# Attention followed by a spectral mixing layer: one prefetched weight tile per stage, and the first output unit's last products whole

## The chip, the cores and the metric

The kernel runs on one core of a Trainium2 chip. The metric is the device time of one execution in microseconds (us), from the first to the last instruction and what the device adds around them. The kernel before takes 450.63 us, the median of three runs (450.61 to 451.6); the profiled execution spans 448.3 us.

## The reference, cut to what matters

Two layers run in one launch. The first is attention with a sliding window of 128 and a bias that falls off with distance, for 8 batches, 8 heads, 576 tokens and 64 channels per head. The second takes the result x (8 x 576 x 512), goes to the frequency domain along the tokens, multiplies each of the 64 lowest modes by its own complex 512 x 512 matrix, comes back, adds x, and puts a last 512 x 512 product through a ReLU.

```python
scores = scale * np.matmul(q, k.transpose(0, 1, 3, 2))
scores = np.where(mask, scores + bias[None], -1000000000.0)
...
x = attn_out.transpose(0, 2, 1, 3).reshape(B, S, H * D)
X = np.fft.rfft(x, axis=1)
Xr, Xi = np.real(X[:, :64]), np.imag(X[:, :64])
Yr = np.einsum('bmd,mde->bme', Xr, w_r) - np.einsum('bmd,mde->bme', Xi, w_i)
Yi = np.einsum('bmd,mde->bme', Xr, w_i) + np.einsum('bmd,mde->bme', Xi, w_r)
Y[:, :64] = Yr + 1j * Yi
y = np.fft.irfft(Y, n=S, axis=1)
u = x + y
out = u + np.maximum(u @ w_ch, 0.0)
```

The weights w_r and w_i are 2 x 64 matrices of 1.05 MB each in f32. One of them (the imaginary part of mode 0) has no effect and is not loaded, so 127 are read, and each is used once. The inputs q, k and v together are 28.3 MB.

## The kernel before

The attention is a software pipeline of 16 units (batch, half of the heads). In each stage, the parts of several units run side by side. Three loads per unit (q, k and v, f32) come on the queue of SP; each raw buffer has two places, and the load of unit u + 2 is ordered right after the cast of unit u:

```python
def cast(self, u, w):
    src = self.loaded.pop((w, u))
    if w == "v":
        ...
            nc.vector.tensor_copy(self.vb[u % 2][...], src[row, :2])
        nc.vector.tensor_copy(self.vt[u % 2][64:96, :, :, :D], src[64:96, 2])
    else:
        ...
        nc.vector.tensor_copy(dst.rearrange("p j e d -> p e j d"), src)
    self.load(w, u + 2)
```

While the attention runs, the first weights are already fetched. They come on the queue of GpSimd (POOL), which casts them to bf16 on the way. A gate keeps them from all coming at once: POOL copies one element of the attention's result of the stage before into a small tile, and so waits for it before it orders the next weights. `AHEAD` says how many tiles are ordered behind the gate of a stage. `LATER` adds tiles at the end, into the raw buffers that q, k and v no longer need.

```python
AHEAD = {1: 1, 2: 1, 4: 2, 5: 1, 7: 1, 8: 1, 10: 1, 11: 1, 12: 2, 13: 2}
LATER = {13: 2, 14: 2, 15: 3}
EARLY, NWA, NWB, AGAIN = 14, 6, 2, 8
...
    if stage in AHEAD:
        if stage:
            b, g = at.units[stage - 1]
            nc.gpsimd.tensor_copy(gate[:1, :1], x[:1, b, 0, 256 * g : 256 * g + 1])
        load_w(AHEAD[stage], early, True)
    if stage in LATER:
        load_w(LATER[stage], None, True)
```

One early tile is loaded before the stages, so with the 13 of `AHEAD` there are 14, one for each place of the pool `early`.

Then comes the stream: the remaining weights arrive on the queue of SP in f32 (eight of them once more through POOL in bf16), and TensorE multiplies each by the spectrum XC, four products of 512 columns per weight, into `acc`. SP can order the first of them when the attention's buffers, whose place they take, are free.

```python
for a in range(4):
    nc.tensor.matmul(into[...], lhsT=window[a], rhs=w[a], ...)
```

The end turns the last group of modes into rows `yq` (token side) and, through w_ch, `yw` (channel side), patches them with small DMAs into the spectra Z and ZW, and then makes 18 output units. Each unit j has a pair of PSUM tiles `mm` (channel side, goes through the ReLU on ACT into r) and `yy` (token side), and o = yy + r on DVE. For the first units the last rows are added by a product of their own, so that they need not wait for the patch:

```python
def last_rows(ps, j, rows, c=slice(0, DM)):
    st = units[j][1]
    for n in range(2):
        nc.tensor.matmul(ps[:, n, c], lhsT=FM[:, n, st * P : (st + 1) * P],
                         rhs=rows[:, c], start=False, stop=True, skip_group_check=True)

def activate(j):
    if j == 0:
        last_rows(yys[0][0], 0, heads["yq"])
        for c in sides:
            last_rows(mms[0][0], 0, heads["yw"], c)
    elif j in FIRST:
        last_rows(mms[j][0], j, heads["yw"])
    else:
        begin(j)
        channels(j)
    ...
        nc.scalar.activation(r[:, c], mm[:, c], AF.Relu)
```

`begin(j)` and `channels(j)` start the pair `mm` (4 products from XW, lines 717 of the profile, then 4 from ZW, line 638). `add_tokens` and `finish_tokens` do the same for `yy` (lines 766 and 775). The last rows and the order of the first units before:

```python
zls = [zps.tile([P, DM], FP32, tag=f"z{i}", name=f"zl{i}") for i in range(2)]
for ets in ((0, 1), (2, 3)):
    for zl, c in zip(zls, sides):
        for et in ets:
            nc.tensor.matmul(zl[:, c], lhsT=yT[:, et], rhs=wch[:, et, c],
                             start=(et == 0), stop=(et == 3))
for zl, c, copy in zip(zls, sides, (nc.scalar.copy, nc.vector.tensor_copy)):
    copy(yw[:, c], zl[:, c])
...
activate(0)
...
take(1)
begin(1)
channels(1)
channel_rows = partial(patch, rows=yw, g=LAST, dst=lambda b: ZW[:, b // 2, 1])
channel_rows([(nc.sync, 0), (nc.sync, 1)] + [(nc.gpsimd, b) for b in range(2, B)])
...
for step in ("f0 a1 f1 a2 a3 f2 a7 f7 a9 a5 ...").split():
    {"a": activate, "f": finish}[step[0]](int(step[1:]))
```

Of the kernel before, what the change touches and what calls it, by code (L numbers as in the profile page):

```python
# [10 lines left out]
FP32 = mybir.dt.float32  # L11
# [4 lines left out]
PSUM = bass.MemoryType.PSUM  # L16
# [4 lines left out]
P = 128  # L21
# [20 lines left out]
    ("mask", 1, 0), ("value", 1, 1), ("evacuate", "k", -1), ("mask", 0, 0), ("exp", 3, 0),  # L42
    ("transpose", "q", -2), ("evacuate", "q", -2), ("score", 1, -1), ("norm", 1, 1),
)


class _Halves:


    def __init__(self, tiles):  # L50
        self.tiles = tiles

    def __getitem__(self, key):
        return self.tiles[key[1]][(key[0], *key[2:])]


class _Scratch:
# [352 lines left out]
def kernel(  # L410
# [10 lines left out]
    nc = tc.nc  # L421
    ctx.enter_context(tc.manual_schedule(engines=ALL | {SP}))
    B, H, S, _ = q.shape
    NM, DM, _ = moe_w_r.shape
    AHEAD = {1: 1, 2: 1, 4: 2, 5: 1, 7: 1, 8: 1, 10: 1, 11: 1, 12: 2, 13: 2}
    LATER = {13: 2, 14: 2, 15: 3}
    EARLY, NWA, NWB, AGAIN = 14, 6, 2, 8
    HM = NM // 2
# [41 lines left out]
    with ExitStack() as actx:  # L470
        at = _Attention(tc, actx, q, k, v, (ident, F, FT), x, XC, raw)
        n = len(at.units)
# [50 lines left out]
        for stage in range(min(lags), n + max(lags)):  # L523
# [6 lines left out]
            if stage == 3:  # L530
                at.inverse_table()
# [8 lines that stand above are left out]
    with ExitStack() as mctx:  # L540
# [6 lines left out]
        first = todo_w[0]  # L547
# [4 lines left out]
        ps = pctx.enter_context(tc.tile_pool(name="fps", bufs=1, space=PSUM))  # L552
        heads, free, idle = {}, [], []
# [24 lines left out]
        def late_channels(zw, yT, yw, c):  # L578
            for et in range(4):
                nc.tensor.matmul(zw[:, c], lhsT=yT[:, et], rhs=wch[:, et, c],  # L580
                                 start=(et == 0), stop=(et == 3))
            nc.scalar.copy(yw[:, c], zw[:, c])
# [111 lines left out]
        POOLED, HALVES, FIRST = (3, 4, 9, 11, 13, 14, 15), (0, 1, 2, 3, 7, 12), (0, 1)  # L694
        mms, yys, rs = {}, {}, {}

        def pair(tag, slot=0):
            return heads[tag][slot].tile([P, 2, DM], FP32, tag=tag, name=tag)
# [5 lines left out]

        def begin(j):

            if j not in mms:
                slot = idle.pop(0)
                mms[j] = pair("mm", slot), slot
            mm = mms[j][0]  # L710
            for n in range(2):
                if units[j][1] == FULL:
                    nc.tensor.matmul(mm[:, n], lhsT=pairs, rhs=XW[:, j, n],
                                     start=True, stop=False, skip_group_check=True)
                    continue
                for row in range(2):
                    nc.tensor.matmul(  # L717
                        mm[ROWS[row], n], lhsT=ident[ROWS[n], ROWS[n]],
                        rhs=XW[ROWS[n], j, row], start=True, stop=False, skip_group_check=True,
                    )  # L720

        def channels(j):

            mm, b, st = mms[j][0], *units[j]
            for n in range(2):
                if st == FULL:
                    nc.tensor.matmul(mm[:, n], lhsT=FC, rhs=ZW[:, b // 2 + n, 1],
                                     start=False, stop=True, skip_group_check=True)
                    continue
                for row in range(2):  # L730
                    spread(mm[:, n], row, b + n, 1, st, row)

        def last_rows(ps, j, rows, c=slice(0, DM)):

            st = units[j][1]
            for n in range(2):
                nc.tensor.matmul(ps[:, n, c], lhsT=FM[:, n, st * P : (st + 1) * P],  # L737
                                 rhs=rows[:, c], start=False, stop=True, skip_group_check=True)

        def parts(j):  # L740
            return (slice(0, 1), slice(1, 2)) if j in HALVES else (slice(0, 2),)

        def activate(j):

            if j == 0:
                last_rows(yys[0][0], 0, heads["yq"])
                for c in sides:
                    last_rows(mms[0][0], 0, heads["yw"], c)
            elif j in FIRST:
                last_rows(mms[j][0], j, heads["yw"])  # L750
            else:
                begin(j)
                channels(j)
            mm, slot = mms.pop(j)
            r = rs[j] = heads["out"].tile([P, 2, DM], FP32, tag="r", name="r")
            for c in (0, 1) if j == 0 else parts(j):
                nc.scalar.activation(r[:, c], mm[:, c], AF.Relu)  # L757
            idle.append(slot)
            if j in POOLED:
                nc.gpsimd.tensor_tensor(out=r, in0=r, in1=token_tiles(j), op=ALU.add)  # L760
# [25 lines left out]
        def finish(j):  # L786

            b, st = units[j]
            if j > 0:
                if j not in yys:  # L790
                    take(j)
                if j not in POOLED:
                    add_tokens(j)
                finish_tokens(j)
            (yy, slot), r = yys.pop(j), rs.pop(j)
            o = heads["out"].tile([P, 2, DM], FP32, tag="o", bufs=5, name="o")
            for c in parts(j):
                nc.vector.tensor_tensor(out=o[:, c], in0=yy[:, c], in1=r[:, c], op=ALU.add)  # L798
                if st < FULL:
                    nc.sync.dma_start(  # L800
                        out=out[b + c.start : b + c.stop, st * P : (st + 1) * P].rearrange(
                            "b p e -> p b e"),
                        in_=o[:, c],
                    )
                    continue
                for n in range(c.start, c.stop):
                    nc.sync.dma_start(
                        out=out[b + 2 * n : b + 2 * n + 2, FULL * P :].rearrange("h p e -> p h e"),
                        in_=o[:, n],
                    )  # L810
            free.append(slot)
# [5 lines left out]
        for g in range(NM // 4):  # L817
# [5 lines left out]
            for i in range(8):  # L823
                m, ri = 4 * g + i // 2, i % 2
# [3 lines left out]
                if g == LAST and i == 7:  # L828
                    pctx.close()
                    head = mctx.enter_context(  # L830
                        tc.tile_pool(name="hps", bufs=1, space=PSUM, reuse_waits="tile"))
                    hctx = mctx.enter_context(ExitStack())
                    first = hctx.enter_context(
                        tc.tile_pool(name="h0ps", bufs=1, space=PSUM, reuse_waits="tile"))
                    heads.update(mm=[], yy=[head])
                    free.append(0)
                    mms[0] = _Halves([first.tile([P, DM], FP32, tag=f"m{n}", name=f"m{n}")
                                      for n in range(2)]), 0
                    begin(0)
                    channels(0)  # L840
                    take(0)
                    add_tokens(0)
                    finish_tokens(0)
# [5 lines left out]
                for a in range(4):  # L849
                    nc.tensor.matmul(  # L850
                        into[32 * (i // 2) : 32 * (i // 2) + 32],
                        lhsT=window[a],
                        rhs=w[a],
                        start=(ri == 0 and a == 0), stop=(ri == (m > 0) and a == 3),
# [7 lines left out]
                if k == K1 - 1:  # L862
# [8 lines left out]
                    wch = right.tile([P, 4, DM], BF16, name="wch")  # L871
# [4 lines left out]
                    FM = right.tile([P, 2, 2 * P], BF16, name="FM")  # L876
# [37 lines left out]
        yq, yT = heads[LAST]  # L914
        zctx = ExitStack()
        zps = zctx.enter_context(tc.tile_pool(name="zps", bufs=1, space=PSUM))
        zl = zps.tile([P, DM], FP32, tag="z0", name="zl")
        nc.tensor.matmul(zl, lhsT=ident, rhs=wch[:, 0], start=True, stop=True)
        sides = (slice(0, DM // 2), slice(DM // 2, DM))
# [9 lines left out]
        patch([(nc.sync, 0), (nc.sync, 1)], yq, LAST, lambda b: Z[:, b])  # L929
        patch([(nc.sync, 2)] + [(nc.gpsimd, b) for b in (3, 4, 5, 6)], yq, LAST, lambda b: Z[:, b], 6)  # L930
        yw = F[:, : DM // (2 * NM)].rearrange("p a b -> p (a b)")
        zls = [zps.tile([P, DM], FP32, tag=f"z{i}", name=f"zl{i}") for i in range(2)]
        for ets in ((0, 1), (2, 3)):
            for zl, c in zip(zls, sides):
                for et in ets:
                    nc.tensor.matmul(zl[:, c], lhsT=yT[:, et], rhs=wch[:, et, c],  # L936
                                     start=(et == 0), stop=(et == 3))
        for zl, c, copy in zip(zls, sides, (nc.scalar.copy, nc.vector.tensor_copy)):
            copy(yw[:, c], zl[:, c])
        zctx.close()  # L940
        lctx.close()
        last = mctx.enter_context(
# [3 lines left out]
        heads["yy"].append(last)  # L946
        idle.append(1)
        free.append(1)
        activate(0)
        hctx.close()  # L950
        heads["mm"].insert(0, mctx.enter_context(
            tc.tile_pool(name="mps", bufs=1, space=PSUM, reuse_waits="tile")))
        take(1)
        begin(1)
        channels(1)
# [1 line left out]
        channel_rows([(nc.sync, 0), (nc.sync, 1)] + [(nc.gpsimd, b) for b in range(2, B)])  # L957
        patch([(nc.gpsimd, 7)], yq, LAST, lambda b: Z[:, b], 6)

        for step in ("f0 a1 f1 a2 a3 f2 a7 f7 a9 a5 f3 f5 a4 f9 a6 a11 f6 f4 a10 a14 f10 "  # L960
                     "a15 f11 a8 f14 f8 a13 f15 a16 f16 f13 a17 f17 a12 f12").split():
            {"a": activate, "f": finish}[step[0]](int(step[1:]))

# [29 lines left out]
```

## Time and profile before

| | |
|---|---|
| time, median of three runs | 450.63 us (450.61 to 451.6) |
| span of the profiled execution | 448.3 us |
| PE busy | 358.4 us (80%) |
| DVE, ACT, POOL busy | 178.0, 152.1, 73.4 us |
| mean granted clock of TensorE | 0.893 |
| DMA, bytes on the queues | 157.03 MB, mean 350 GB/s |
| HBM read, written | 162.53 MB, 9.44 MB |
| attention | from the start to about 143 us |
| stream of the weights | first product at 143.9 us, last at 412.6 us |
| output units | from there to 448 us |

The profile has a strip of 40 slices of 11.2 us each; a digit is the busy share in tenths. A view by stretches gives the same as numbers for any window: busy time of each engine with the count of its instructions, then the granted clock (1.00 is full), the DMA share (the time of all packets over 16 engines; two packets in work on one engine count twice, so it can pass 1), and GB/s as the queues count them. The waits name the engine that waited, for whom, the sum in us, how often, and the longest. In a timeline, a line begins with its start and its length in us, and the brackets at its end hold the idle time before it and what ended it.

### The profile page before, as it was taken

Reading aid. Unit: us, or ns where it says so; the run is one execution under the profiler, and the core shown is the slowest. Engines: PE = TensorE matmul, PEld = TensorE weight load, DVE = VectorE, ACT = ScalarE, POOL = GpSimd, SP = SyncE. Lnnn points to the kernel's source line nnn. Section 1 sums busy time; section 2 is a strip of 40 time slices with the busy share of each in tenths; the row PEclk is TensorE's granted clock in tenths of the full one; section 3 lists DMA queues with packets and bytes.
Section 4 is the critical chain, followed back from the end, with each engine's and each line's share of the span. In section 5 each row is a group of like instructions: output and inputs, shape, how many; then the busy total and the mean of one; then the engine's idle time right before and its main releaser. Section 6 shows DMA issues by size and latency. Waiting matters only on the chain. (4 is left out here: it accounts for less than half of the span.)

```text
span 448.3 us, 8025 instructions
## 1 busy us (share of the span) xinstructions
PE 358.4 (80%) x3316; PEld 194.1 (43%) x3316; DVE 178.0 (40%) x324; ACT 152.1 (34%) x195; POOL 73.4 (16%) x129
## 2 busy tenths in 40 slices
PE   4679899999947866556776867999999998867993
PEld 3357677777636532212221323444454443323331
DVE  7689699999742211010010223121212202211684
ACT  6759799999930000000000011111221110110772
POOL 8610101011300300200000000000000000064781
PEclk8679899999985996786666699999999999999998
DMA  8999999999999999999999999999999999994597
GB/s 281 304 323 306 303 253 298 329 312 283 233 215 330 354 289 316 335 383 426 419 423 421 422 421 420 421 420 417 423 420 419 422 418 421 422 400 157 206 358 291
DMA packets 53767, 157.03 MB, mean 350 GB/s; under 512 B 5204, under 2 KB 24420, under 8 KB 41316
## 3 DMA queue, kind: packets, MB, share of 16 engines
q1 hardware_dynamic: 47908, 140.56, 81.2%
q0 software_dynamic: 5824, 15.97, 18.0%
q8 instruction: 26, 0.43, 0.4%
q14 instruction: 9, 0.07, 0.0%
HBM read 162.53 MB, written 9.44 MB: 384 GB/s over the span
## 5 line engine op out<-in xcount | busy, mean ns | idle before, releaser
L850 PE MATMUL acc<-w,XC 128*32 128x512 bf16 x456 | 128.5, 445 | 46.0 <-DMA w<-in_moe_w_i_dram 28.4
L850 PEld LDWEIGHTS <-XC 128*32 128x32 bf16 x508 | 59.2, 139 | 116.3 <-issue 83.7
L304 ACT ACTIVATE att<-sc 128x1024 bf16<-128x1024 f32 x64 | 64.1, 1032 | 10.0 <-PE sc L294 10.0
L615 ACT CAST ZW<-zw 128x512 bf16<-128x512 f32 x8 | 4.7, 585 | 150.7 <-PE zw L613 150.7
L341 PE MATMUL av<-vb,att 128*128 128x132 bf16 (+1 forms) x576 | 41.5, 227 | 11.2 <-DVE x L357 7.1
L341 PEld LDWEIGHTS <-att 128*128 128x128 bf16 x704 | 39.7, 104 | 16.8 <-DVE x L357 11.5
L587 DVE TENSOR_SCALAR yq<-acc 128x512 bf16<-128x512 f32 x13 | 8.9, 688 | 92.8 <-PE acc L850 92.7
L628 POOL DMA_DIRECT2D Z<-yq x19 | 9.7, 519 | 214.8 <-issue 208.7
L690 ACT CAST XW<-my 128x512 bf16<-128x512 f32 x36 | 19.3, 589 | 75.4 <-PE my L638 75.4
L662 DVE COPY xT<-tr 128x1024 bf16<-128x1024 bf16 x18 | 12.5, 692 | 69.7 <-PE tr L660 69.7
L681 PE MATMUL my<-wch,xT 128*64 128x512 bf16 x288 | 34.5, 382 | 0.8 <-DVE xT L662 0.8
L266 ACT COPY qkT<-tp 128x1152 bf16<-128x1152 bf16 x30 | 33.5, 1115 | 4.1 <-PE tp L260 3.4
L294 PE MATMUL sc<-qkT 64*64 64x256 bf16 (+2 forms) x640 | 25.6, 267 | 2.5 <-ACT qkT L266 1.6
L357 DVE TENSOR_TENSOR x<-av,rec 128x640 bf16<-128x640 f32 x32 | 26.4, 825 | 1.1
L243 DVE CAST vb<-vr 64x1024 bf16<-64x1024 f32 x32 | 22.7, 708 | 5.7 <-DMA vr<-in_v_dram 5.4
L798 DVE TENSOR_TENSOR o<-yy,r 128x512 f32<-128x512 f32 (+1 forms) x24 | 21.8, 953 | 5.5 <-ACT r L757 3.6
L294 PEld LDWEIGHTS <-qkT 64*64 64x64 bf16 x640 | 14.7, 110 | 19.5 <-issue 16.2
L681 PEld LDWEIGHTS <-xT 128*64 128x64 bf16 x288 | 14.8, 109 | 18.9 <-issue 6.9
L281 PE MATMUL sc<-bias,ident 128*128 128x512 bf16 x64 | 20.4, 401 | 1.6 <-ACT att L304 1.6
L617 DVE CAST Z<-z 64x512 bf16<-64x512 f32 x16 | 11.0, 689 | 24.4 <-PE z L610 24.3
L315 DVE TENSOR_TENSOR att<-att,mask 128x1024 bf16<-128x1024 bf16 x32 | 20.6, 684 | 0.0
L757 ACT ACTIVATE r<-mm 128x1024 f32<-128x1024 f32 (+1 forms) x22 | 17.2, 829 | 7.5 <-PE mm L638 4.9
(139 smaller groups left out, 368.1 us busy)
## 6 DMA issues: line engine op xcount, KB each, us to landing
w<-in_moe_w_i_dram SPq DMA_DIRECT2D x52, 1024.0 KB, 18.0
w<-in_moe_w_r_dram SPq DMA_DIRECT2D x45, 1024.0 KB, 17.9
qr<-in_q_dram SPq DMA_DIRECT2D x16, 576.0 KB, 7.0
kr<-in_k_dram SPq DMA_DIRECT2D x16, 576.0 KB, 7.9
vr<-in_v_dram SPq DMA_DIRECT2D x64, 128.0 KB, 6.8
w<-in_moe_w_r_dram POOLq DMA_DIRECT2D x16, 512.0 KB, 10.2
out_dram<-o SPq DMA_DIRECT2D x10, 512.0 KB, 3.8
out_dram<-o SPq DMA_DIRECT2D x16, 256.0 KB, 3.6
```

The source lines that it names most:

```text
L243: nc.vector.tensor_copy(self.vb[u % 2][row, :, :, :, W * half : W * half + D], src[row, :2])
L266: (self.nc.vector.tensor_copy if u < 2 and w == "q" else self.nc.scalar.copy)(dst.rearrange("q h (p j) -> q h p j", j=TPP), tp.rearrange(" ...
L281: nc.tensor.matmul(sc[:, e], lhsT=self.ident, rhs=self.bias[:, hv].rearrange("p j n -> p (j n)"), start=True, stop=False, skip_group_check ...
L294: nc.tensor.matmul(sc[64 * half : 64 * half + 64, e, j * 256 + c0 : j * 256 + c0 + n], lhsT=qkT[row, 1, h, k0 + j : k0 + P : 2], rhs=qkT[r ...
L304: self.nc.scalar.activation(self.att[u % 2][:, kt * 8 * P : (kt + 1) * 8 * P], sc.rearrange("p e n -> p (e n)"), AF.Exp, scale=1.0 / math. ...
L315: nc.vector.tensor_tensor(out=rows, in0=rows, in1=self.table[:, heads], op=ALU.mult)
L341: nc.tensor.matmul(bank[:, qt * W : qt * W + rhs[j].shape[1]], lhsT=att[:, o : o + P], rhs=rhs[j], start=(n == 0 and j == 0), stop=(n == l ...
L357: nc.vector.tensor_tensor(out=self.x[:, b, :, cs].rearrange("p t (h d) -> p h t d", h=2), in0=tiles[:, :, :, :D], in1=rec.unsqueeze(-1).br ...
L681: nc.tensor.matmul(mm[ROWS[half]], lhsT=lhsT, rhs=wch[:, dt], start=(dt == 0), stop=False, skip_group_check=True,)
L690: nc.scalar.copy(XW[:, j, n], mms[n])
L798: nc.vector.tensor_tensor(out=o[:, c], in0=yy[:, c], in1=r[:, c], op=ALU.add)
L850: nc.tensor.matmul(into[32 * (i // 2) : 32 * (i // 2) + 32], lhsT=window[a], rhs=w[a], start=(ri == 0 and a == 0), stop=(ri == (m > 0) and ...
```

## The change

Two things change. In the attention, the 13 weight tiles behind gates are spread evenly: one behind the gate of each of stages 1 to 13. Before, stages 3, 6 and 9 ordered none and stages 4, 12 and 13 two each. It is meant to keep the transfers even, so that stages with two tiles do not hold up the loads of q, k and v.

At the end, the special treatment of output unit 0 is taken away. Its pair `mm` is one tile of two PSUM banks as for any other unit (it was two tiles, so that each half could be activated by itself). The last channel rows are made one half of the columns after the other, with both copies on ACT. And unit 0 is activated after unit 1 has been started, with the token-side rows of unit 0 added in `finish(0)`.

```diff
-    AHEAD = {1: 1, 2: 1, 4: 2, 5: 1, 7: 1, 8: 1, 10: 1, 11: 1, 12: 2, 13: 2}
+    AHEAD = {stage: 1 for stage in range(1, 14)}
...
         def activate(j):
-            if j == 0:
-                last_rows(yys[0][0], 0, heads["yq"])
-                for c in sides:
-                    last_rows(mms[0][0], 0, heads["yw"], c)
-            elif j in FIRST:
+            if j in FIRST:
                 last_rows(mms[j][0], j, heads["yw"])
...
-            for c in (0, 1) if j == 0 else parts(j):
+            for c in parts(j):
                 nc.scalar.activation(r[:, c], mm[:, c], AF.Relu)
...
         def finish(j):
-            if j > 0:
+            if j == 0:
+                last_rows(yys[0][0], 0, heads["yq"])
+            else:
...
-                    heads.update(mm=[], yy=[head])
-                    free.append(0)
-                    mms[0] = _Halves([first.tile([P, DM], FP32, tag=f"m{n}", name=f"m{n}")
-                                      for n in range(2)]), 0
+                    heads.update(mm=[head], yy=[head])
+                    idle.append(0)
+                    free.append(0)
...
-        zls = [zps.tile([P, DM], FP32, tag=f"z{i}", name=f"zl{i}") for i in range(2)]
-        for ets in ((0, 1), (2, 3)):
-            for zl, c in zip(zls, sides):
-                for et in ets:
-                    nc.tensor.matmul(zl[:, c], lhsT=yT[:, et], rhs=wch[:, et, c],
-                                     start=(et == 0), stop=(et == 3))
-        for zl, c, copy in zip(zls, sides, (nc.scalar.copy, nc.vector.tensor_copy)):
-            copy(yw[:, c], zl[:, c])
+        for i, c in enumerate(sides):
+            zl = zps.tile([P, DM], FP32, tag=f"z{i}", name=f"zl{i}")
+            late_channels(zl, yT, yw, c)
...
-        activate(0)
-        hctx.close()
-        heads["mm"].insert(0, mctx.enter_context(
-            tc.tile_pool(name="mps", bufs=1, space=PSUM, reuse_waits="tile")))
         take(1)
         begin(1)
         channels(1)
...
-        for step in ("f0 a1 f1 a2 a3 f2 a7 f7 a9 a5 f3 f5 a4 f9 a6 a11 f6 f4 a10 a14 f10 "
+        for step in ("a0 f0 a1 f1 a2 a3 f2 a7 f7 a9 a5 f3 f5 a4 f9 a6 a11 f6 f4 a10 a14 f10 "
```

More of the change, by code (lines that the diff above doesn't have):

```diff
@@ L44 @@
 )
[L47 to L54, printed above, removed]
 class _Scratch:
@@ L705, in begin @@
         def begin(j):
[L707 to L710, printed above, removed]
+            slot = idle.pop(0)
+            mm = pair("mm", slot)
+            mms[j] = mm, slot
             for n in range(2):
@@ L731, in channels, with last_rows @@
                     spread(mm[:, n], row, b + n, 1, st, row)
-        def last_rows(ps, j, rows, c=slice(0, DM)):
+        def last_rows(ps, j, rows):
             st = units[j][1]
             for n in range(2):
-                nc.tensor.matmul(ps[:, n, c], lhsT=FM[:, n, st * P : (st + 1) * P],
-                                 rhs=rows[:, c], start=False, stop=True, skip_group_check=True)
+                nc.tensor.matmul(ps[:, n], lhsT=FM[:, n, st * P : (st + 1) * P], rhs=rows,
+                                 start=False, stop=True, skip_group_check=True)
         def parts(j):
@@ L831 @@
                         tc.tile_pool(name="hps", bufs=1, space=PSUM, reuse_waits="tile"))
-                    hctx = mctx.enter_context(ExitStack())
-                    first = hctx.enter_context(
-                        tc.tile_pool(name="h0ps", bufs=1, space=PSUM, reuse_waits="tile"))
-                    heads.update(mm=[], yy=[head])
+                    heads.update(mm=[head], yy=[head])
+                    idle.append(0)
                     free.append(0)
-                    mms[0] = _Halves([first.tile([P, DM], FP32, tag=f"m{n}", name=f"m{n}")
-                                      for n in range(2)]), 0
                     begin(0)
```

## The prediction

> **What bounds the kernel now.** I read the 40-slice strip first, then the stretches, the waits, and the end of the timeline. In the strip the two DMA rows carry the case:
>
> ```profile
> PE   4679899999947866556776867999999998867993
> DMA  8999999999999999999999999999999999994597
> GB/s 281 304 323 306 303 253 298 329 312 283 233 215 330 354 289 316 335 383 426 419 423 421 422 421 420 421 420 417 423 420 419 422 418 421 422 400 157 206 358 291
> ```
>
> The DMA row reads 9 from the second slice to the 36th, so from about 11 to 403 us all 16 DMA engines have work. PE is full only in slices 4 to 10. The GB/s row drops to 215 in places, which looks like room. The stretches show that it is not (columns: the stretch and its length, busy time of PE, weight load, DVE, ACT, POOL, the clock, DMA share, GB/s):
>
> ```profile
> 4.00:8.00 4.00, 1.45 (x19) 1.01 (x18) 3.68 (x9) 3.13 (x5) 3.84 (x6) 0.94 1.04 391
> 9.00:12.00 3.00, 1.42 (x16) 0.97 (x17) 2.17 (x3) 2.10 (x4) 2.83 (x6) 0.50 1.16 262
> 51.00:59.00 8.00, 7.71 (x139) 6.26 (x134) 6.44 (x13) 7.31 (x9) 1.54 (x3) 0.94 1.00 251
> 65.60:72.20 6.60, 6.24 (x120) 5.02 (x119) 6.49 (x13) 6.37 (x9) 0.02 (x1) 1.00 0.98 314
> 86.20:92.80 6.60, 6.21 (x108) 4.36 (x110) 6.01 (x12) 6.11 (x7) 0.01 (x1) 1.00 1.10 341
> 120.00:127.00 7.00, 5.99 (x114) 4.47 (x108) 1.76 (x4) 5.97 (x9) 0.00 (x0) 1.00 1.06 213
> 190.00:396.00 206.00, 172.00 (x964) 74.98 (x962) 36.66 (x74) 24.01 (x44) 1.70 (x4) 0.90 1.02 419
> ```
>
> From 4 to 8 us nearly all that moves is q and k (packets of 2304 bytes): 391 GB/s at a full share. From 9 to 12 nearly all is v (512 bytes): 262 GB/s with a little else beside it, about 250 for v alone, also full. From 190 to 396 only f32 weights move: 419. From 120 to 127 the queue carries weights that are cast to bf16 on the way; the column counts what is written, so 213 is 426 GB/s of reading. A low figure is therefore the price of the packets, not room. The page agrees: 162.53 MB are read from HBM, while the queues' totals count a cast weight (1.05 MB read) at half.
>
> A price list follows: v 250, q and k 390, weights 422 GB/s. I sorted the packets by size within each stretch. From 120 to 139 us, 0.03 MB of v and 7.99 MB of weights cost 0.1 + 18.9 = 19.1 us of 19.0. From 28.5 to 35.5, 0.59 of v, 0.94 of q and k and 0.95 of weights cost 2.4 + 2.4 + 2.3 = 7.0 of 7.0. So the time until the last weight lands (about 411 us) is **the DMA's work plus its idle time**. PE and the attention only matter where they leave the DMA without orders.
>
> The longest wait on a load in the attention stands in the waits as:
>
> ```profile
> DVE vb L243 <- DMA vr<-in_v_dram: 5.4, 2, 4.9
> ```
>
> Its 4.9 us end at 127.2 us: the cast of v for the last unit. That load was issued at 110.6 to 112.6 us, among two cast weights of stage 12 (issued 106.7 and 107.3), two of stage 13 and four behind them (113.3 to 115.9). PE then stands still from 126.5 to 131.4 us and restarts at half clock. It looks like 5 us to win, but the DMA share is 1.06 all through it.
>
> **What the Trainium skill says.** In "DMA: Bandwidth & Descriptors", section "Queues, rings and completion order", each DMA engine takes turns between the queues it has work for, packet by packet. The trace agrees: from 118 to 129 us the last few v packets trickle through at 4 to 5 GB/s beside 205 to 211 of cast weights. "Where 436 GB/s comes from" on the same page gives 435 GB/s as the ceiling and about 358 for the HBM of one core; this trace holds 419 for 206 us, so the second figure does not bind here and the first nearly does. In "TensorE: Matmul & The Clock Gate", section "What's actually happening", the clock halves after an idle window of about 3.4 us. The stretch 127 to 139 us agrees, with a mean clock of 0.64 after 4.9 us of idling.
>
> **The change, part by part.** First, the prefetch. Weights, casts and their number stay: 13 tiles behind gates in both. Counted up to each stage 1 to 13, before has issued 1,2,2,4,5,5,6,7,7,8,9,11,13 and after 1 to 13 in turn. One tile moves from stage 4 to 3, and two of those at stages 12 and 13 are in effect issued from stage 6 and 9 on. POOL makes three more one-element gate copies of 0.57 us, 1.7 us on an engine that is 16% busy: nothing.
>
> Per stage, the orders are 1.18 MB of q and k and 0.59 of v, 3.0 + 2.4 = 5.4 us at these prices, and 2.5 us for each weight tile (1.05 / 422). Stages last 6.2 to 8 us (gates 28.5, 35.5, 51.0, 59.1, 72.2, 79.7, 92.8, 99.1, 106.2, 112.8). So a stage without a tile leaves the DMA about 1.4 us of room, one with a tile asks for 7.9 and pushes work on, one with two asks for 10.4. Where was it really short of work? Cost against time between the gates:
> - 43 to 51: 8.3 of 8.0, none (the backlog of stage 2 is served).
> - 51 to 59: 0.18 of v, 1.13 of q and k, 1.26 of weights: 0.7 + 2.9 + 3.0 = 6.6 of 8.0, **1.4 us lost**, at 52 to 55 us, while stage 4's two tiles were only starting.
> - 65.6 to 72.2: 2.4 + 3.6 + 0.2 = 6.3 of 6.6, **0.3 lost** (the share is 0.98, and 1.0 or more in every other row).
> - 86.2 to 92.8: 2.6 + 4.0 + 0.2 = 6.7 of 6.6, none.
>
> A tile ordered at stage 3 lies in the queue when the hole at 52 comes; one at stage 6 fills the hole at 70. That is 1.7 us at most. I take 1.1 as the gain, since the price list has an error of some tenths per stretch and part of a hole may move. All later weights then land 1.1 us sooner, and so does the last one.
>
> The stall of the last unit should shrink by most of its 4.9 us: with one tile fewer at stage 12, v of the last unit meets little other traffic between 110.6 and 113. PE should then keep its clock, and the first streamed product come several us before 143.9. I count **nothing** for it: from 112 to 396 us the DMA never pauses in either case.
>
> Second, the end. Before, the two halves of the last channel rows are made in the order of the half transposes (8 products of 256 columns, 413.94 to 415.08), copied by ACT (414.94, 0.37 us) and DVE (415.11, 0.42 us), and unit 0's products stand ahead of unit 1's start:
>
> ```profile
> 414.91 0.59 PE L737 MATMUL yy<-yq,FM 128*128 128x512 bf16 x2
> 415.36 0.61 PE L737 MATMUL m<-F,FM 128*128 128x256 bf16 x4
> 415.90 0.41 PE L717 MATMUL mm<-XW,ident 64*64 64x512 bf16 x4
> 416.14 0.39 PE L638 MATMUL mm<-ZW,FT 64*64 64x512 bf16 x4
> 416.46 0.60 PE L737 MATMUL mm<-F,FM 128*128 128x512 bf16 x2
> ```
>
> After, one half is finished whole before the other, so ACT can copy the first at about 414.6 and the second at 415.1 to 415.5; two copies on one engine cost nothing against 415.53. Then PE runs unit 1's start first (0.34 + 0.22 us: 415.6 to 416.15), then unit 0's two pairs (0.43 each). Unit 0's first activation moves from 415.90 to about 416.6, **0.7 us later**, and PE loses the 0.43 us of yy products that used to lie in the shadow of the copies.
>
> But the next units wait for something else:
>
> ```profile
> 419.04 0.40 PE L638 MATMUL mm<-ZW,FT 64*64 64x512 bf16 x2 [0.25 <-DMA ZW<-F]
> ```
>
> The rows of ZW that unit 2 reads are written by a small DMA, issued at 416.60 on SP once unit 1's products (until 416.5) have read the old rows. In the new order these are done at about 416.15, so that DMA starts some 0.4 us sooner and lands at about 418.6. PE gets there after 416.15 + 5 pairs x 0.43 + 0.34 + small gaps = 418.7. So both paths meet again at unit 2, at 418.7 instead of 419.04 at best, and a few tenths later if unit 0's later activation holds a buffer. I count +0.2 us with an error of 0.5.
>
> Sum of the time: 450.63 - 1.1 + 0.2 = **449.7 us**.
>
> **Rivals.**
> - The stall was on the path: the time falls by 4.9 us plus what the half clock costs, to about 443 to 446. For it: PE really stands, and the stream's first tiles wait for buffers that the attention frees (the second is issued at 139.05). Against it: 422 GB/s of reading at that very time; an earlier stream only takes the place of the backlog.
> - The even order asks 7.9 us of the DMA in stages of about 6.8, eleven times in a row from stage 3. Loads of q, k and v come later, PE waits in the middle, and with a shorter backlog behind stage 13 the DMA could run dry before the stream's buffers are free: at 139 us only some 1 to 1.5 MB were still queued, less than the two tiles moved. Then the 1.1 us is given back and the time is 450.5 to 452. Against it: the last unit's v arrives sooner, so the buffers come free sooner too.
> - The end loses what the halves had won: 0.7 us reaches the last output, 450.2 to 450.8. For it: from 414 to 431 us the chain of waits is nearly all PE, so an added gap is kept; against it the landing at 419.0.
>
> **Range and chances.** The gain is bounded by the 1.7 us of holes, the loss by the halves' 0.7 and a dry spell of 1 to 2 us. That gives 448.2 to 451.0. Two per cent would be 9.0 us; only the first rival comes near it, and no rival loses that much: 2% faster, 97% the same, 1% slower.
>
> **What the new profile would show.** DMA share 1.0 or more in every stretch from 43 to 396 us, the holes at 52 and 70 gone; the wait of vb for vr far under 4.9 us; the stream's first product several us before 143.9 while the last weight lands only about 1 us sooner; unit 0's activation about 0.7 us later after the last weight product, and the ZW wait of PE gone or shorter. I am wrong if the DMA share falls under 1 between 125 and 145 us, or if the time from the last weight product to the end changes by more than 0.7 us.

## The result, and the profile after

The changed kernel takes 448.57 us (median of six runs, 448.27 to 449.23) against 450.94 of the kernel before in the same comparison: ratio 0.9954, 95% interval 0.9938 to 0.9969. That is 2.1 us less, with 1.4 to 2.8 inside the interval. In a later comparison, with 22 runs of it, the ratio was 0.9974 (0.9960 to 0.9988), 1.2 us less. The profiled execution spans 446.6 us (before 448.3).

The strip of the changed kernel, its two DMA rows:

```profile
DMA  8999999999999999999999999999999999994697
GB/s 283 323 322 317 302 316 294 309 287 291 213 214 343 315 317 315 339 388 425 420 421 420 421 423 420 420 420 418 422 420 419 420 418 422 422 395 171 226 357 274
```

The slices between 45 and 101 us (the fifth to the ninth) now stand at 302, 316, 294, 309 and 287 where they were 303, 253, 298, 329 and 312: the dip of the sixth is gone. The stretches of the changed kernel (the same columns as before, the DMA share and GB/s last):

```profile
51.00:59.00 8.00, 7.71 (x141) 6.24 (x138) 6.93 (x15) 7.72 (x9) 1.05 (x2) 1.00 1.09 299
65.60:72.20 6.60, 6.24 (x123) 4.99 (x112) 5.70 (x11) 6.44 (x8) 1.04 (x2) 1.00 1.09 298
86.20:92.80 6.60, 5.22 (x96) 3.76 (x87) 3.80 (x7) 5.78 (x6) 0.71 (x2) 1.00 1.06 292
112.00:120.00 8.00, 7.94 (x121) 6.71 (x118) 5.30 (x11) 4.31 (x7) 3.10 (x6) 0.79 0.96 215
120.00:127.00 7.00, 6.09 (x113) 4.29 (x102) 5.72 (x11) 6.52 (x8) 0.53 (x1) 1.00 1.06 211
190.00:396.00 206.00, 174.41 (x962) 75.38 (x962) 36.66 (x74) 24.36 (x45) 3.33 (x7) 0.87 1.02 419
```

Read the last two numbers of each row. At 51 us the share went from 1.00 to 1.09, at 65.6 from 0.98 to 1.09: both holes are filled in this profile. In the row at 86.2 PE does less than before (5.22 us against 6.21): the attention is held up, above all by q, as the waits below show. And at 112 us stands a share of 0.96: a new hole. From 190 us on nothing has changed, 419 GB/s.

The wait of v's cast in the changed kernel:

```profile
DVE vb L233 <- DMA vr<-in_v_dram: 1.3, 1, 1.3
```

So 1.3 us where 4.9 was the longest. With q it is the other way round (20 to 145 us; first the kernel before, then the changed one):

```profile
DVE q L248 <- DMA qr<-in_q_dram: 0.8, 1, 0.8
```

```profile
DVE q L238 <- DMA qr<-in_q_dram: 6.0, 4, 2.0
```

The even order was meant to keep the loads from being held up; those of q it holds up more. Of the 6.0 us, 4.6 lie between 83 and 116 us, where the kernel before has none. Stage 8's gate opens 3.0 us sooner than before (76.69 us against 79.72), but stage 13's opens 2.8 us later (first the kernel before):

```profile
112.83 0.51 POOL L535 COPY gate<-x 1x1 bf16<-1x1 bf16 x1 [5.02 <-DVE x L357]
```

```profile
115.58 0.51 POOL L525 COPY gate<-x 1x1 bf16<-1x1 bf16 x1 [7.05 <-DVE x L347]
```

The first streamed product starts at 139.48 us (before 143.88), the last weight's four products at 410.33 (before 411.86). From there to the end of the last sum it is 30.36 us (before 31.04). The gain of this pair of profiles is thus 1.53 us in the stream and 0.68 us after it.

The PE and ACT rows of the end in the changed kernel, then the SP rows of the ZW patch, first of the changed kernel, then of the kernel before:

```profile
412.41 1.15 PE L570 MATMUL zl<-wch,xT 128*128 128x256 bf16 x8
413.49 0.41 PE L706 MATMUL mm<-XW,ident 64*64 64x512 bf16 x4
413.73 0.39 PE L628 MATMUL mm<-ZW,FT 64*64 64x512 bf16 x4
414.05 0.60 PE L726 MATMUL mm<-F,FM 128*128 128x512 bf16 x2
416.55 0.68 PE L628 MATMUL mm<-ZW,FT 64*64 64x512 bf16 x4
```

```profile
413.21 0.77 ACT L572 CAST F<-zl 128x256 bf16<-128x256 f32 x2 [1.08 <-issue]
414.69 2.07 ACT L742 ACTIVATE r<-mm 128x512 f32<-128x512 f32 x4 [0.72 <-DMA Z<-yq]
```

```profile
414.36 1.25 SPq L618 DMA_DIRECT2D ZW<-F  x2
```

```profile
416.60 1.26 SPq L628 DMA_DIRECT2D ZW<-F  x2
```

Unit 1's start (413.49) follows the rows' products at once, while ACT is still copying them (413.21 to 413.98). The patch of ZW is ordered 414.36 - 410.33 = 4.03 us after the last weight's products began; before it was 416.60 - 411.86 = 4.74. PE's wait for ZW (0.25 us at 419.04 before) no longer stands in the changed kernel's waits.

### The profile page after: what moved, and what is told of

It reads as the page before. It is cut to its first block, busy times and chain, and to the rows that moved or that the text cites. A ratio compares the mean times of both kernels' runs of the same rounds, so it can differ in the third digit from the quotient of the medians.

```text
span 446.6 us, 8026 instructions
## 1 busy us (share of the span) xinstructions
PE 354.3 (79%) x3314; PEld 190.9 (43%) x3314; DVE 177.9 (40%) x323; ACT 152.3 (34%) x196; POOL 74.7 (17%) x132
## 5 line engine op out<-in xcount | busy, mean ns | idle before, releaser
L833 PE MATMUL acc<-w,XC 128*32 128x512 bf16 x456 | 126.5, 466 | 48.5 <-DMA w<-in_moe_w_i_dram 34.2
L833 PEld LDWEIGHTS <-XC 128*32 128x32 bf16 x508 | 58.3, 140 | 116.9 <-issue 89.0
L331 PE MATMUL av<-vb,att 128*128 128x132 bf16 (+1 forms) x576 | 38.8, 218 | 12.9 <-DVE x L347 8.0
L331 PEld LDWEIGHTS <-att 128*128 128x128 bf16 x704 | 37.0, 99 | 18.4 <-DVE x L347 12.4
L742 ACT ACTIVATE r<-mm 128x512 f32<-128x512 f32 (+1 forms) x24 | 18.1, 811 | 7.4 <-PE mm L628 4.1
```

What stands on the lines that cost most here:

```text
L331: nc.tensor.matmul(bank[:, qt * W : qt * W + rhs[j].shape[1]], lhsT=att[:, o : o + P], rhs=rhs[j], start=(n == 0 and j == 0), stop=(n == l ...
L833: nc.tensor.matmul(into[32 * (i // 2) : 32 * (i // 2) + 32], lhsT=window[a], rhs=w[a], start=(ri == 0 and a == 0), stop=(ri == (m > 0) and ...
```

## Experiments

**Theory:** the last weight lands when the DMA has done its work, so only lost DMA time counts, and the even order fills two holes; the new end is 0.7 us shorter on its own. **Rivals:** the stall of the last unit was on the path; the evenness of the order is what counts, because it keeps the loads flowing; all of the gain lies in the end.

The table has one profile of each kernel. Lost time is the stretch 4 to 165 us minus its packets (each counted where it ends) at the price list of the prediction, as a difference to the kernel before (whose own figure is -0.9: the prices are a little high, and only differences count). The ratios leave disturbed runs out, so they are not quite the quotients of the medians.

| kernel | DMA time lost to 165 us | first streamed product | last weight's products | from there to the last sum | median us, ratio (95%) |
|---|---|---|---|---|---|
| before | 0 | 143.88 | 411.86 | 31.04 | |
| changed | -1.2 | 139.48 | 410.33 | 30.36 | 448.57, 0.9954 (0.9938 to 0.9969) |
| changed, again | -0.9 | 138.28 | 410.01 | 30.36 | 449.09, 0.9974 (0.9960 to 0.9988) |
| even prefetch, old end | -1.1 | 138.26 | 410.40 | 31.04 | 449.69, 0.9983 (0.9967 to 0.9999) |
| uneven, new end | -0.6 | 139.94 | 410.82 | 30.37 | 450.02, 0.9989 (0.9963 to 1.0015) |
| uneven, unit 1 first | -1.1 | 134.41 | 410.92 | 30.54 | 449.20, 0.9961 (0.9939 to 0.9983) |
| one tile 4 to 3 | -2.3 | 133.18 | 408.79 | 30.37 | 448.73, 0.9949 (0.9927 to 0.9972) |
| the same, again | -0.9 | 137.15 | 410.32 | 30.36 | 449.16, 0.9989 (0.9967 to 1.0012) |
| tiles at 6 and 9 | +0.8 | 140.35 | 411.73 | 30.35 | 450.57, 1.0001 (0.9974 to 1.0028) |
| none up to 6 | +11.4 | 147.17 | 423.69 | 30.36 | 462.15, 1.0245 (1.0192 to 1.0298) |
| two at 12, no gate at 13 | +5.7 | 149.63 | 416.68 | 30.37 | 454.40, 1.0071 (1.0046 to 1.0097) |
| two at 12, gate kept | -2.5 | 138.17 | 408.49 | 30.35 | 448.19, 0.9967 (0.9949 to 0.9986) |
| all by stage 7 | +6.9 | 150.11 | 418.37 | 30.35 | 455.60, 1.0092 (1.0051 to 1.0134) |
| tile of 9 to 12 | -1.8 | 140.46 | 409.75 | 30.36 | 447.61, 0.9946 (0.9926 to 0.9966) |

**Even prefetch alone.** The kernel before with one line changed:

```diff
-    AHEAD = {1: 1, 2: 1, 4: 2, 5: 1, 7: 1, 8: 1, 10: 1, 11: 1, 12: 2, 13: 2}
+    AHEAD = {stage: 1 for stage in range(1, 14)}
```

> Kernel before with the even prefetch alone; the end with unit 0 in halves stays. DMA theory (the landing of the last weight is the DMA's work plus its lost time): the last weight lands 1.5 us sooner as in the changed kernel, the end keeps its length, so 1.5 us less than before, ratio 0.9967. Theory that the end carries the gain: no change, 1.000. Theory that the stall of the last unit was on the path: 0.99 or less, and the end adds nothing.

The last weight's products start 1.46 us sooner and the end keeps its 31.04 us. Timed, it is 0.8 us faster (interval 0 to 1.5): the first theory's direction, at half its size.

**New end alone.** The changed kernel with that line put back.

> Kernel before with the new end alone; prefetch uneven as before. DMA theory with an end that is 0.7 us shorter from the last weight product to the last sum (31.0 to 30.4 us): 0.7 us less, ratio 0.9985, the wait of vb for vr still near 5 us. If the whole gain lies in the prefetch: 1.000.

The end takes 30.37 us, as foretold; the ratio 0.9989 cannot be told from 1, so the end's gain is shown by the profiles and not by the timing. This profile, with the same uneven prefetch as before, has its last weight 1.0 us sooner than the kernel before, and v's longest wait is 2.3 us, not the 5 expected. The hole of 51 to 59 us costs 0.6 us here where it cost 1.4. So executions of one prefetch order differ by about 1 us, and a pair of profiles cannot settle a gain of 1.5. Three profiles each do better: uneven 411.86, 410.82 and 410.92 (mean 411.20), even 410.33, 410.40 and 410.01 (mean 410.25), **0.95 us** for the prefetch. With only three of each its size is rough (standard error 0.35 us).

**One tile from stage 4 to 3 only**, with 12 and 13 still at two:

```diff
-    AHEAD = {stage: 1 for stage in range(1, 14)}
+    AHEAD = {1: 1, 2: 1, 3: 1, 4: 1, 5: 1, 7: 1, 8: 1, 10: 1, 11: 1, 12: 2, 13: 2}
```

> New end; of the prefetch only one tile moved, from stage 4 to stage 3; stages 6 and 9 still none, 12 and 13 still two. DMA theory: the hole at 52 to 55 us is filled and that at 70 stays, so some 1.2 us come sooner out of the stream, and the stall of 4 to 5 us at v of the last unit remains; with the end 1.9 us less than before, ratio 0.9958. Theory that the stall is on the path: only the end's 0.7 us, 0.9985.

**Tiles at 6 and 9 only**, with 4 still at two:

```diff
+    AHEAD = {1: 1, 2: 1, 4: 2, 5: 1, 6: 1, 7: 1, 8: 1, 9: 1, 10: 1, 11: 1, 12: 1, 13: 1}
```

> New end; stage 4 still two and stage 3 none, but one tile each at 6, 9, 12 and 13. DMA theory: the hole at 52 stays, that at 70 is filled (0.3 us), and a new one at 112 to 119 us takes up to 1 us back, so the stream ends 0 to 0.7 us later than before though the stall of the last unit is gone; with the end -0.7 to 0 us, ratio 0.9985 to 1.000. Theory that the stall is on the path: most of the gain is here, 0.995 or less.

These two part the theories. The second has no wait of v's cast left and streams its first product 3.5 us sooner than the kernel before (140.35), yet its last weight comes only 0.13 us sooner and its time is the same. The stall was not on the path. Its holes, in the stretch view:

```profile
51.00:59.00 8.00, 7.56 (x133) 5.96 (x132) 6.46 (x13) 7.60 (x10) 1.49 (x4) 0.98 1.05 275
112.00:120.00 8.00, 6.47 (x120) 5.24 (x119) 6.76 (x13) 6.73 (x9) 2.15 (x5) 1.00 0.97 229
```

The first row keeps a hole (0.75 us at these prices), the second has the new one (0.67): the queue has run out of weights before the gate of stage 13 opens. The first kernel has neither and is among the fastest; its last weight comes 3.1 us sooner where 1.2 was expected, of which more below. But it also has no stall to speak of (0.2 us of waiting), though I had expected 4 to 5: the crowd at stages 12 and 13 does not force it.

**No tile up to stage 6**, then two a stage:

```diff
+    AHEAD = {7: 1, 8: 2, 9: 2, 10: 2, 11: 2, 12: 2, 13: 2}
```

> New end; no tile behind a gate in stages 1 to 6, one at 7, two at each of 8 to 13. DMA theory: without a tile a stage of some 6.8 us has 5.2 to 5.4 us of work, so 1.4 to 1.7 us are lost in each of six stages, some 8 to 9 us from 28 to 70 us, where the kernel before lost 1.4 net; with the end that is 6 to 7 us more than before, ratio 1.013 to 1.017, and the DMA share falls under 1 up to 70 us. Theory that only the crowd at stages 12 and 13 counts (stall at v of the last unit): about as before, 0.998 to 1.005.

```profile
51.00:59.00 8.00, 7.71 (x143) 6.13 (x137) 7.45 (x14) 7.64 (x9) 0.00 (x0) 1.00 0.67 199
```

PE does the same 7.71 us of work in this stretch as before, so the attention is not disturbed, but the share is 0.67: this is what an idle DMA looks like. The loss came larger than foretold, 11.4 us of DMA time; the last weight comes 11.8 us later and the time is 11 us longer. From 20 to 79.7 us it is 10.2 us more than before, where 8 to 9 less 1.4 were expected. From 28.5 to 72.2 us this kernel loses 9.7 us, but not evenly: 3.5 of them lie at 51 to 59 us and 0.9 to 1.8 in each other stretch between the gates of the kernel before. Another 1.0 is lost up to 79.7 us, behind the stage with one tile.

**Two at stage 12 and nothing at 13**, first without the gate of 13:

```diff
+    AHEAD = {**{stage: 1 for stage in range(1, 12)}, 12: 2}
```

> Changed kernel with the tile of stage 13 moved to stage 12 (one each at 1 to 11, two at 12). DMA theory: the new hole of the even order at 112 to 119 us (0.7 us at these prices, 1.1 with the stretch before it) is filled, the last weight lands 0.5 to 1 us sooner than in the changed kernel, ratio to before about 0.993. Theory that evenness counts: as slow as the changed kernel or slower, 0.995 to 0.998.

The expectation failed: 3.2 us slower than before. The stretch, then the POOL and SP rows of this kernel:

```profile
127.00:139.00 12.00, 5.94 (x80) 5.34 (x81) 7.54 (x14) 2.20 (x3) 1.59 (x3) 0.57 0.57 119
```

```profile
109.54 0.54 POOL L451 DMA_DIRECT2D w<-in_moe_w_r_dram  x1
110.06 0.72 POOL L451 DMA_DIRECT2D qr<-in_moe_w_i_dram  x1
110.96 0.53 POOL L451 DMA_DIRECT2D qr<-in_moe_w_r_dram  x1 [0.18 <-DMA vr<-in_v_dram]
111.48 0.54 POOL L451 DMA_DIRECT2D kr<-in_moe_w_i_dram  x1
```

```profile
114.50 10.19 SPq L208 DMA_DIRECT2D vr<-in_v_dram  x4
```

The weights into the raw buffers of q and k have no gate of their own. Here they follow the second tile of stage 12 directly, five weights in 2.5 us (the first of them, not shown, at 109.02), and all lie ahead of the last unit's v, whose four orders take SP 10.2 us. DVE then waits 8.6 us for v, the attention ends 10 us later than in the changed kernel, and when what is queued is through, only one more weight is ordered (at 131.68) before the stream's first at 140.53: a share of 0.57 for 12 us.

To part the missing gate from the second tile, the gate was kept without a tile of its own (`12: 2, 13: 0`):

> As the run with two tiles at stage 12 and none at 13, but the gate of stage 13 stays (a copy with no tile of the pool behind it), so the tiles into the raw buffers still wait for stage 13. If the missing gate made that run slow, by letting weights into the queue ahead of v of the last unit: the dry spell at 128 to 140 us (5.6 us at these prices) is gone and the time is that of the changed kernel or up to 1 us less, ratio 0.993 to 0.996. If the second tile at stage 12 made it slow: 1.003 or more, with the dry spell still there.

```profile
115.62 0.51 POOL L525 COPY gate<-x 1x1 bf16<-1x1 bf16 x1 [5.41 <-DVE x L347]
116.13 0.53 POOL L451 DMA_DIRECT2D qr<-in_moe_w_i_dram  x1
```

The weights into q's raw buffer are ordered at 116.13 instead of 110.06, the dry spell is gone, and 448.19 us stand against 454.40. It was the gate. The ratio, 0.9967, is just above the range expected; against the changed kernel in the same comparison (449.09 us) the gain can't be told from none.

**All 13 tiles by stage 7:**

```diff
+    AHEAD = {1: 2, 2: 2, 3: 2, 4: 2, 5: 2, 6: 2, 7: 1}
```

> New end; all 13 tiles early: two at each of stages 1 to 6, one at 7, none after. DMA theory: the backlog lasts through the later stages, no hole, nothing lost up to 165 us though q, k and v come late and PE waits for them; the last weight lands as soon as in the kernel with one tile moved to stage 3, or sooner, ratio 0.995 or less. Theory that bursts hold up the attention and that this costs: attention ends several us later and the time is that of before or longer, 1.000 to 1.01.

The expectation failed again, and most usefully. The stretches:

```profile
43.00:59.00 16.00, 9.75 (x196) 7.75 (x186) 8.07 (x15) 8.73 (x10) 1.93 (x4) 0.91 1.07 286
104.00:112.00 8.00, 7.42 (x138) 5.93 (x137) 7.84 (x16) 7.73 (x9) 0.00 (x0) 1.00 0.86 249
127.00:139.00 12.00, 10.91 (x203) 8.51 (x198) 9.48 (x18) 10.88 (x12) 1.15 (x3) 1.00 0.84 173
```

At 43 us the DMA is full but PE has 9.75 us of work in 16: the bursts do hold up q, k and v. No DMA time is lost there. But the attention ends later (first streamed product at 150.11), and by then the tiles have long run out, so the DMA has too little to do at 104 and at 127 us. I read it as a late attention that costs once the backlog is gone. This run doesn't part the two: the kernel with no tile up to stage 6 shows that stages without a tile lose time even where the attention is not disturbed.

**Halves kept, unit 1 first.** The kernel before, with unit 1's start and the patch of ZW moved ahead of `activate(0)` (the lines that close and open PSUM pools move along and are left out here):

```diff
-        activate(0)
...
         take(1)
         begin(1)
         channels(1)
         channel_rows([(nc.sync, 0), (nc.sync, 1)] + [(nc.gpsimd, b) for b in range(2, B)])
+        activate(0)
```

> Kernel before (uneven prefetch, unit 0 in halves, two copies on two engines), but unit 1 is started ahead of unit 0's last products. If the order made the new end shorter: from the last weight product to the last sum 30.4 to 30.5 us, as in the changed kernel, since the rows of ZW are read sooner and patched sooner. If the halves themselves cost the time: 31.0 us as before. The stream is that of before, ratio 0.9985 or 1.000.

The end takes 30.54 us: 0.50 of the 0.68 us come from the order. The other 0.18 come with the rest of the new end (the whole pair, one half of the rows after the other, both copies on ACT); this run doesn't part those. The half-width products are not the price: four of them take 0.44 us in the chain, two whole ones 0.43. The 0.18 lie in unit 2's ZW products, 0.70 us in the chain here and 0.51 in the changed kernel. The ratio, 0.9961 (0.9939 to 0.9983), is lower than either expectation: of the 1.8 us the end explains 0.5. In the profile the last weight came 0.9 us sooner, though the prefetch is that of before; one order varies by that much, and the rest of the gain in time stays unexplained.

**The changed kernel and the one-tile kernel again, and a better order** (none at 9, two at 12, one at 13, gates else as they are):

```diff
+    AHEAD = {stage: 1 + (stage == 12) for stage in range(1, 14) if stage != 9}
```

> The changed kernel again, on the same chip as the other three: ratio to before 0.9954 as measured first, within 0.9938 to 0.9969; a hole near 112 to 119 us again if it belongs to the schedule and not to that one execution.

> The kernel with only one tile moved to stage 3 (stages 6 and 9 none, 12 and 13 two), again beside the changed kernel. If it is better than the even order, as its 1.1 us less of lost DMA time says: 0.993, 1 us under the changed kernel. If its profile was a lucky one: the same as the changed kernel, 0.995, with a stall at v of the last unit and some lost time.

> Changed kernel with the tile of stage 9 moved to stage 12 (none at 9, two at 12, one at 13, all other gates as they are). DMA theory: stage 9 has enough backlog, the hole at 112 to 119 us is filled by the second tile of stage 12, and the last weight lands up to 1 us sooner than in the changed kernel, ratio 0.993. Theory that only full evenness keeps the loads flowing: 0.996 or more.

The changed kernel came out at 0.9974, just outside its first interval. Its new hole was 0.3 us this time, against 0.65 before and 0.8 in the kernel with the even prefetch alone. The one-tile kernel did not repeat its 408.79, so its first profile was a lucky one. Its two ratios, 0.9949 and 0.9989, also show that ratios from different comparisons can't be ranked within 0.4%. The kernel with the tile moved from stage 9 to 12 has no loss at 112 to 120 us and the lowest ratio, 0.9946. Beside the changed kernel in the same comparison its mean is 1.1 us lower (95% interval 0.5 to 1.7), so it is probably better. Not only the second tile does it: without a tile at stage 9 DVE waits only 0.9 us for q from 83 to 116 us, and stage 13's gate opens at 113.56.

## Why the prediction was right, and where it was wrong

**What bounds the kernel: right.** Over the 14 profiles the start of the last weight's products follows the lost DMA time with a slope of 1.04 and a correlation of 0.996, from -2.5 to +11.4 us. Without the three large losses the correlation is 0.94, and single profiles miss the line by up to 0.7 us. In part this is bookkeeping: all kernels move the same bytes, so lost time counts what is still unmoved at 165 us. What the traces add is that nothing made it up later, in the changed kernel 419 GB/s from 190 to 396 us as before. The price list finds the loss where the share alone does not: at 51 us the kernel before has a share of 1.00 and loses 1.4 us (1.1 if each packet is counted where it starts). The strip was misread in one place: PE is full in the 26th to the 33rd slice too, 88.7 us of the 90 from 280 to 370. The DMA still moves 420 GB/s there, and at 409 us PE waits for a weight again, so the bound holds.

**The stream, -1.1 us: right in size.** Measured 1.5 by one pair of profiles, 0.95 by three of each, 0.8 by the timing of the prefetch alone. The terms behind it were not those of the sum, so the good size is partly luck. The hole of 1.4 us belonged partly to that one execution (0.6 and 0.5 in the two other uneven profiles). And of the 1.2 us by which the first pair differs, about 1.0 is there by 40 us, up to where both kernels order the same. From there on the means of three profiles each say: the even order gets 1.6 us ahead by 106.2 us, and gives 0.9 back by 120 us. The sum had no term for giving back; it only took 1.1 of the 1.7 us to be careful.

**"The DMA never pauses from 112 us": wrong.** The even order pauses at 112 to 120 us, for 0.3 to 0.8 us. With the backlog of the double stages gone, the queue ran dry before stage 13 opened its gate, and that gate opened late (115.6 to 115.8 us in the three even profiles, 112.0 to 112.8 in the three uneven ones). The prediction's second rival had this, with q, k and v late and PE waiting in the middle; its dry spell was placed at 125 to 145 us and came earlier, and small. Leaving aside the three orders that lost over 5 us, the pattern holds in every profile. The five with a tile at both 6 and 9 wait 3.5 to 5.5 us for q from 83 to 116 us and open that gate at 115.6 to 117.9. The six with none at 9 wait 0.9 us at most and open it at 110.7 to 113.6. Nor did PE keep its clock in the changed kernel: it stands for 2.0 us before 111.77, less than the prediction goes by, and the clock is at half from 112.3 to 115.7 us.

**The stall is worth nothing: right**, as the kernel with tiles at 6 and 9 shows; the one with the lowest ratio still waits 2.9 us for v. Its cause as I gave it, the crowd of stages 12 and 13, is open: three more kernels with the same crowd had waits of v's cast of 2.3 us or less, and what makes it long in one execution was not found. The packets of the kernel before show only how slow v is in a crowd: from 111 to 114 us it moves 157 packets of 512 bytes beside 142 of 4096 bytes of the cast weights, so 25 to 29 GB/s where it had 250 alone. The last few, from 118 us on, come at 1.5 to 5.6 GB/s (the prediction has 4 to 5).

**The end, +0.2 us: wrong in sign; it was -0.68, just inside the 0.7 set as a sign of being wrong.** The failed step is "Then PE runs unit 1's start first ... 415.6 to 416.15", behind the copies. PE ran it in their shadow, 3.16 us after the last weight's products began, where I had 3.74. In the program unit 1's start, which needs no copy, now stands right behind the rows' products. So the yy products lost their place in the shadow, but unit 1's start took it. The ZW patch came 0.71 us sooner, not 0.4, and unit 0's activation 0.32 us later (414.69 - 410.33 = 4.36 against 415.90 - 411.86 = 4.04), not 0.7. The mechanism, ZW's old rows read sooner so that unit 2 waits less, was the right one: at the end of unit 2's ZW products the changed kernel is already 0.7 us ahead, counted from the rows' products on.

The sum, -0.9, thus missed 0.9 us at the end of the kernel. With 0.95 and 0.68 it is -1.6 us, between the two timings (-2.1 and -1.2). The first timing, 448.57, lies near the lower end of the range forecast.

## What to carry to other kernels

Price each kind of packet in a stretch where it runs alone, and compare a stage's orders with its time: in this case that found lost DMA time where the share still said 1. When DMA is the bound, PE stalls in front of it cost only if the queue then runs dry, so what a prefetch order has to keep is a backlog at each gate, above all at the last ones. An even order is not by itself a gentle one: here a tile at both stages 6 and 9 went with late loads of q and a late last gate. A gate that seems to guard one transfer may also hold back those ordered behind it.

## What was not expected of the hardware

With the same prefetch order, the last weight came at times 1.0 to 1.5 us apart from one profile to the next (410.82 to 411.86 uneven, 408.79 to 410.32 with one tile moved), as much as the change itself. And with five cast weights in the queues, four orders of 128 KB on SP took 10.2 us to issue, where the kernel before needs about 1.9 us for the last unit's four: the wait for v began in issuing it.
